# Gated mix of two linear-attention blocks: the key and value projections in five column runs instead of eight

## The chip, the cores and the metric

The kernel runs on one core of one Trainium2 chip. The metric is the device time of one execution in microseconds, as the median of several runs; lower is better.

## The reference

The input x has 2048 rows and 576 columns. Two linear-attention blocks, A and B, of 32 heads of 18 columns each read it, and a sigmoid gate mixes their outputs.

```python
def _A_ref(x, wqkv, wo):
    q, k, v = ...                      # x @ wqkv, split into 32 heads of 18
    phi = lambda t: jnp.where(t > 0, t + 1, jnp.exp(t)) + 1e-6
    pq, pk = phi(q), phi(k)
    kv = jnp.einsum("bhsd,bhse->bhde", pk, v)
    z = jnp.einsum("bhsd->bhd", pk)
    num = jnp.einsum("bhqd,bhde->bhqe", pq, kv)
    den = jnp.einsum("bhqd,bhd->bhq", pq, z)[..., None] + 1e-6
    return (num / den) ... @ wo

def _B_ref(x, wqkv, w_phi, wo):
    q, k, v = ...
    pq = jnp.einsum("bhsd,hdf->bhsf", q, w_phi)
    pk = jnp.einsum("bhsd,hdf->bhsf", k, w_phi)
    phi_q = jnp.concatenate([_softmax(pq), _softmax(-pq)], axis=-1)
    phi_k = jnp.concatenate([_softmax(pk), _softmax(-pk)], axis=-1)
    ...                                # kv, z, num, den as in A, with phi_q and phi_k

g = _sigmoid((x * gate_w).sum(-1, keepdims=True))
return g * a + (1 - g) * b
```

## The kernel before

**Tiles.** x is cut into 16 tiles of 128 rows. The host hands over x transposed, the inner dimension of 576 as five blocks of 128 (`KT`; the fifth block holds the last 64 rows twice). Every operand of a projection is split into a high part in f32r and the rest, also in f32r. `load_x` loads a tile, copies it to `xh` on ScalarE (L104) and takes the difference `xl` on GpSimd (L105). `split` does the same for a weight block: copy on ScalarE (L115), difference on VectorE or GpSimd (L117), the raw block in one of three buffers `wraw` (at the start also in halves of the three `uw` buffers).

**A projection.** `proj` (L149 to L157) adds 14 matmuls into one PSUM region: for each of the first four blocks high x times high weight, high times low, low times high, and for the fifth block, whose doubled rows hold both weight parts, two. Each has 128 rows of x as stationary operand, loaded anew, and 288 columns of a weight as moving operand. A run of columns is thus 14 matmuls.

**The key/value part.** For each tile come four projections of 576 columns, each in two runs of 288: value A, key A, key B, value B, with the weights `WAv`, `WAk`, `WBk`, `WBv` in four of five equal buffers of the pool `wp`. `WBk` is key B's weight already multiplied by `w_phi`; `fold_w` makes it on TensorE (L142) in five groups of heads, and ScalarE and VectorE write it out (L144 to L147). The values land in PSUM tiles `tr` of one bank, and ScalarE copies them into `vt` (buffer name `vo`, L233, two buffers, one a tile). The keys land in `pq`, two banks with 288 columns in each. Key A goes through `phi_elu` (ScalarE L173, VectorE L174 and L175). Key B goes through `softmax_exp`: VectorE finds maxima and minima by head and subtracts (L180, L181, L187, L188), ScalarE takes the exponential (L189), VectorE adds up by head and inverts (L191, L193); `scale_uw` then multiplies on GpSimd (L198).

**The sums.** `kv_a` and `kv_b` (L212) add the products of values and mapped keys of a tile into the two PSUM banks `bk`, which stay open over all 16 tiles. For tile t-1 they stand, in the written order, behind value A and key A of tile t. Tiles 0 and 1, and 14 and 15, have an order of their own, written out by hand.

**The query part.** It follows for the same 16 tiles, with `WBq` (folded at tile 3), `WAq`, the output weights `WoB` and `MA`, and the transposed mapped queries `uwt`, all from the same pool of five weight buffers: a later weight takes the buffer of the weight that is done. It has its own matmuls (L157 by way of `q_units`, L348, L428 to L442 transposes, L460, L490).

**What sets the order.** The kernel's text gives priorities. A scheduler places every instruction on its engine's queue by a model of the times, so the matmuls of neighbouring runs may be interleaved. Each engine then runs its queue in order and waits by semaphores. All transfers are issued on the SyncE queue (SP).

Of the kernel before, what the change touches and what calls it, by code (L numbers as in the profile page):

```python
# [11 lines left out]
ALU = mybir.AluOpType  # L12
# [11 lines left out]
VC = DH + 1  # L24
EPS = 1e-6


@with_exitstack
def tile_gated_mix(ctx, tc, xT, wAk, wAv, wBv, wAq, wkT, wqT, phi, woA, woB, out):
# [9 lines left out]
    def r(ap):  # L39
        return ap.bitcast(F32)  # L40

    def pq_tile():
        return ps.tile([P, 2, 512], F32, name="pq")

    def tr_tile():
        return ps.tile([P, 512], F32, name="tr")
# [59 lines left out]
        return xh, xl  # L106


    def w_tile():
        return wp.tile([P, 9, 578], F32R, name="W")  # L110

    def split(src, hi, lo, eng=V, raw=None):
        raw = (wraw_tile() if raw is None else raw)[:src.shape[0], :src.shape[1]]
        nc.sync.dma_start(raw, src)
        A.activation(hi, raw, AF.Copy)  # L115
        a = P - lo.shape[0] if hi.shape[0] == P else 0
        eng.tensor_tensor(lo, raw[a:], r(hi[a:]), op=ALU.subtract)  # L117

    def load_w(src, n, eng=V, raws=(None,) * KT):
        W = w_tile()  # L120
        for j in range(4):
            split(src[:, j, :], W[:, j, :n], W[:, 5 + j, :n], eng, raws[j])
        split(src[:, 4, :], W[:, 4, :n], W[64:, 4, :n], eng, raws[4])
        return W

    def fold_w(src):
        W = w_tile()
        ph = row_tile()
        nc.sync.dma_start(ph[:126, :630], phi)
        for g, nh in GROUPS:  # L130
            n = nh * DH
            c = slice(126 * g, 126 * g + n)
# [10 lines left out]
            p1v = p1[:, :504].rearrange("p (i c) -> p i c", c=126)[:, :, :n]  # L143
            A.activation(W[:, 0:4, c], p1v, AF.Copy)  # L144
            A.activation(W[:, 4, c], p2[:, :n], AF.Copy)
            V.tensor_tensor(W[:, 5:9, c], p1v, r(W[:, 0:4, c]), op=ALU.subtract)
            V.tensor_tensor(W[64:, 4, c], p2[64:, :n], r(W[64:, 4, c]), op=ALU.subtract)  # L147
        return W

    def proj(dst, x, W, c0, n):  # L150
        xh, xl = x
        steps = []
        for j in range(4):
            steps += [(xh, j, j), (xh, j, 5 + j), (xl, j, j)]
        steps += [(xh, 4, 4), (xl, 4, 4)]
        for i, (xx, j, w) in enumerate(steps):
            PE.matmul(dst, xx[:, j, :], W[:, w, c0:c0 + n], start=(i == 0), stop=(i == len(steps) - 1))  # L157

    def halves(p):
        return p[:, :, :HB]  # L160

    def heads(p):
        return p[:, :, :HB].rearrange("p a (h d) -> p a h d", d=DH)

    def bc2(t):
        return t.rearrange("p (a h) -> p a h", a=2)[:, :, :, None].to_broadcast([P, 2, 16, DH])


    def phi_elu(pq):
        f = row_tile()  # L170
        fx = f[:, :D]
        fv = fx.rearrange("p (a b) -> p a b", a=2)
        A.activation(fv, halves(pq), AF.Exp)  # L173
        V.tensor_scalar(fx, fx, 1.0, EPS, op0=ALU.min, op1=ALU.add)  # L174
        V.scalar_tensor_tensor(fv, halves(pq), 1.0 + EPS, fv, op0=ALU.add, op1=ALU.max)  # L175
        return f

    def softmax_exp(pq):
        mm = sm.tile([P, 64], F32, name="mm")
        V.tensor_reduce(mm[:, :32], heads(pq), op=ALU.max, axis=AX.X)  # L180
        V.tensor_reduce(mm[:, 32:], heads(pq), op=ALU.min, axis=AX.X)  # L181
        uw = uw_tile()

        def v4(s):
            return uw[:, s, :].rearrange("p (a h d) -> p a h d", a=2, d=DH)

        V.tensor_tensor(v4(0), heads(pq), bc2(mm[:, :32]), op=ALU.subtract)  # L187
        V.tensor_tensor(v4(1), bc2(mm[:, 32:]), heads(pq), op=ALU.subtract)  # L188
        A.activation(uw, uw, AF.Exp)  # L189
        ss = sm.tile([P, 64], F32, name="ss")  # L190
        V.tensor_reduce(ss, uw.rearrange("p s (h d) -> p (s h) d", d=DH), op=ALU.add, axis=AX.X)  # L191
        rs = sm.tile([P, 64], F32, name="rs")
        V.reciprocal(rs, ss)  # L193
        return uw, rs
# [34 lines left out]
    def do_v(t, x, W, which):  # L229
        for hf in range(2):  # L230
            pv = tr_tile()
            proj(pv[:, :HB], x, W, HB * hf, HB)
            A.activation(vt[t % 2][:, which, 16 * hf:16 * hf + 16, :DH],  # L233
                         pv[:, :HB].rearrange("p (h d) -> p h d", d=DH), AF.Copy)

    def do_pq(x, W, n=D):
        pq = pq_tile()
        proj(pq[:, 0, :HB], x, W, 0, HB)
        proj(pq[:, 1, :n - HB], x, W, HB, n - HB)
        return pq  # L240

    def do_ak(x):
        return phi_elu(do_pq(x, WAk))

    def do_bk(x, eng=G):
        uw, rs = softmax_exp(do_pq(x, WBk))
# [5 lines left out]
    WAv = load_w(wAv, D, raws=[None, None, None] + spare[:2])  # L252
    xs[1] = load_x(1)
    do_v(0, xs[0], WAv, 0)
    do_v(1, xs[1], WAv, 0)
    WAk = load_w(wAk, D, raws=spare[2:] + [None])
    f0 = do_ak(xs[0])
    f1 = do_ak(xs[1])
    kv_a(0, f0)
    WBk = fold_w(wkT)  # L260
    WBv = load_w(wBv, D)
    u0 = do_bk(xs[0])
    do_v(0, xs.pop(0), WBv, 1)
    xs[2] = load_x(2)
    kv_a(1, f1)
    u1 = do_bk(xs[1])
    kv_b(0, u0)
    do_v(1, xs.pop(1), WBv, 1)
    pend = (None, u1)
    for t in range(2, NT - 2):  # L270
        x = xs.pop(t)
        do_v(t, x, WAv, 0)
        fa = do_ak(x)
        xs[t + 1] = load_x(t + 1)
        if pend[0] is not None:
            kv_a(t - 1, pend[0])
        kv_b(t - 1, pend[1])
        uw = do_bk(x)
        do_v(t, x, WBv, 1)
        pend = (fa, uw)  # L280
        if t == 3:
            WBq = fold_w(wqT)
# [5 lines left out]
    do_v(t0, x0, WAv, 0)  # L288
    f0 = do_ak(x0)
    kv_a(t0 - 1, pend[0])  # L290
    kv_b(t0 - 1, pend[1])
    do_v(t1, x1, WAv, 0)
    f1 = do_ak(x1)
    kv_a(t0, f0)
    u0 = do_bk(x0)
    do_v(t0, x0, WBv, 1)
    kv_a(t1, f1)
    WAq = load_w(wAq, 578, G)
    u1 = do_bk(x1, V)
    do_v(t1, x1, WBv, 1)  # L300
    kv_b(t0, u0)

    def widths(p):
# [14 lines left out]

    WoB = w_tile()
# [8 lines left out]
    MA = w_tile()  # L330

    def ma_units():
        wos = []
# [25 lines left out]


    def maps_a(pa):
        f = phi_elu(pa)
# [35 lines left out]
    def q_units(t, x=None):  # L398
        x = x or load_x(t)
        pb = pq_tile()  # L400
        proj(pb[:, 0, :HB], x, WBq, 0, HB)
        yield
        proj(pb[:, 1, :HB], x, WBq, HB, HB)
        sb = softmax_exp(pb)
# [137 lines left out]
        return [wk.tile([P, KT, 256], F32R, name=n) for n in ("ath", "atl")]  # L542

    def uwt_tiles():
        u = wp.tile([126, 2, 10, 256], F32R, name="W")
        return u[:, 0], u[:, 1]

    order = [t0, t1] + list(range(NT - 2))
# [82 lines left out]
```

## Time and profile before

| | us |
|---|---|
| median of 3 runs | 625.52 (624.28 to 626.02) |
| the profiled execution | 623.18 |
| its span, first to last instruction | 621.5 |
| TensorE matmul busy, weight loads busy | 604.0, 591.5 |
| VectorE, ScalarE, GpSimd busy | 391.5, 204.7, 174.4 |

PE is TensorE's matmuls and PEld its weight loads, which overlap them; DVE is VectorE, ACT ScalarE, POOL GpSimd, SP SyncE. Matmuls are pipelined: one may start while the one before it still runs, so the time from start to start is what a matmul costs, and the duration of one in the trace holds its latency too. L157 is line 157 of the kernel before. The granted clock of TensorE is 1.000 throughout.

### The profile page before, as it was taken

Reading aid. Unit: us, or ns where it says so; the run is one execution under the profiler, and the core shown is the slowest. Engines: PE = TensorE matmul, PEld = TensorE weight load, DVE = VectorE, ACT = ScalarE, POOL = GpSimd, SP = SyncE. Lnnn points to the kernel's source line nnn. Section 1 sums busy time; section 2 is a strip of 40 time slices with the busy share of each in tenths; the row PEclk is TensorE's granted clock in tenths of the full one; section 3 lists DMA queues with packets and bytes.
Section 4 is the critical chain, followed back from the end, with each engine's and each line's share of the span. In section 5 each row is a group of like instructions: output and inputs, shape, how many; then the busy total and the mean of one; then the engine's idle time right before and its main releaser. Section 6 shows DMA issues by size and latency. Waiting matters only on the chain.

```text
span 621.5 us, 11676 instructions
## 1 busy us (share of the span) xinstructions
PE 604.0 (97%) x5000; PEld 591.5 (95%) x5000; DVE 391.5 (63%) x644; ACT 204.7 (33%) x420; POOL 174.4 (28%) x126
## 2 busy tenths in 40 slices
PE   6999999999999999999998799999999999999997
PEld 6999999999999999999997599999999999999997
DVE  6373353323323332326999998989889988889920
ACT  6342232221222222235333344243332334332331
POOL 6013221112222222245245212434133443312300
PEclk9999999999999999999999999999999999999999
DMA  8441130000000000024011101011010110000001
GB/s 285 124 142 41 44 112 3 21 22 22 22 22 24 22 22 24 22 64 122 22 38 50 35 22 40 22 42 41 20 41 22 41 42 20 20 20 20 16 24 39
DMA packets 12660, 27.94 MB, mean 45 GB/s; under 512 B 1388, under 2 KB 1388, under 8 KB 12608
## 3 DMA queue, kind: packets, MB, share of 16 engines
q1 hardware_dynamic: 12608, 27.19, 14.1%
q8 instruction: 39, 0.64, 0.4%
q14 instruction: 13, 0.11, 0.1%
HBM read 22.47 MB, written 4.72 MB: 44 GB/s over the span
## 4 chain that ended last, share of the span: by engine, by line
PE 82%; DVE 13%; ACT 2%; DMA 2%; issue 1%; SPq 0%; ACTq 0%
PE pq L157 32%; PE tr L157 19%; PE bk L490 16%; PE bk L212 5%; PE tr L460 4%; PE tr L435 2%; DVE row L384 1%; DVE dd L385 1%; DMA wraw<-wBv 1%; DVE uw L198 1%; PE tr L428 1%; DVE W L424 1%; PE pq L142 1%; DVE gg L366 1%; DVE row L175 1%; DVE den L373 1%
## 5 line engine op out<-in xcount | busy, mean ns | idle before, releaser
L157 PE MATMUL pq<-W,xh 128*128 128x288 f32 (+1 forms) x1152 | 254.3, 300 | 0.2 <-DVE den L390 0.2
L157 PEld LDWEIGHTS pq<-W,xh 128*128 128x128 f32 x1152 | 190.9, 189 | 3.1 <-PE tr L348 0.6
L157 PE MATMUL pq<-W,xl 128*128 128x288 f32 (+1 forms) x640 | 187.1, 298 | 0.0
L157 PE MATMUL tr<-W,xh 128*128 128x288 f32 x576 | 124.4, 301 | 5.8 <-ACT W L115 5.3
L105 POOL TENSOR_TENSOR xl<-xraw,xh 128x640 fp32r<-128x640 f32 x29 | 45.4, 1566 | 301.2 <-ACT xh L104 300.6
L157 PEld LDWEIGHTS pq<-W,xl 128*128 128x128 f32 x640 | 120.8, 189 | 0.2
L157 PEld LDWEIGHTS tr<-W,xh 128*128 128x128 f32 x576 | 96.7, 193 | 6.6 <-ACT W L115 5.3
L157 PE MATMUL tr<-W,xl 128*128 128x288 f32 x320 | 93.9, 299 | 0.0
L174 DVE TENSOR_SCALAR row<-row 128x576 f32<-128x576 f32 x32 | 24.4, 762 | 101.2 <-ACT row L173 101.2
L233 ACT ACTIVATE vo<-tr 128x288 f32<-128x288 f32 x64 | 25.9, 407 | 150.2 <-PE tr L157 150.2
L490 PE MATMUL bk<-W,ath 128*128 128x288 f32 x288 | 63.5, 301 | 1.1 <-ACT ath L423 0.7
L191 DVE TENSOR_REDUCE ss<-uw 128x64 f32<-128x1152 f32 x32 | 43.2, 1351 | 31.0 <-ACT uw L189 30.9
L157 PEld LDWEIGHTS tr<-W,xl 128*128 128x128 f32 x320 | 61.8, 193 | 0.0
L490 PE MATMUL bk<-W,vo 126*128 126x288 f32 x384 | 61.3, 299 | 0.0
L490 PEld LDWEIGHTS bk<-W,vo 126*128 126x128 f32 x384 | 54.0, 189 | 0.0
L180 DVE TENSOR_REDUCE mm<-pq 128x32 f32<-128x576 f32 x32 | 23.9, 748 | 47.0 <-PE pq L157 47.0
L189 ACT ACTIVATE uw<-uw 128x1152 f32<-128x1152 f32 x32 | 37.3, 1167 | 41.7 <-DVE uw L188 41.0
L490 PEld LDWEIGHTS bk<-W,ath 128*128 128x128 f32 x288 | 47.2, 189 | 1.5 <-ACT ath L423 0.9
L490 PE MATMUL bk<-W,atl 128*128 128x288 f32 x160 | 47.4, 297 | 0.0
L371 POOL TENSOR_TENSOR row<-row,z_a 128x576 f32<-128x576 f32 x16 | 30.1, 1882 | 52.5 <-DVE row L175 52.5
L460 PE MATMUL tr<-W,kb_h 126*126 126x256 f32 (+1 forms) x160 | 32.4, 283 | 1.0 <-DVE vo L465 0.8
L198 POOL TENSOR_TENSOR uw<-uw,rs 128x1152 f32<-128x1152 f32 x15 | 32.3, 2155 | 0.7 <-DVE rs L193 0.7
(138 smaller groups left out, 875.7 us busy)
## 6 DMA issues: line engine op xcount, KB each, us to landing
xraw<-xT SPq DMA_DIRECT2D x30, 320.0 KB, 3.1
out<-row SPq DMA_DIRECT2D x16, 288.0 KB, 2.1
wraw<-woA SPq DMA_DIRECT2D x6, 288.0 KB, 2.9
wraw<-wAq SPq DMA_DIRECT2D x5, 289.0 KB
wraw<-wBv SPq DMA_DIRECT2D x5, 288.0 KB, 4.2
wraw<-wkT SPq DMA_DIRECT2D x4, 315.0 KB
wraw<-wqT SPq DMA_DIRECT2D x4, 315.0 KB
uw<-wAk SPq DMA_DIRECT2D x4, 288.0 KB
```

The source lines that it names most:

```text
L105: eng.tensor_tensor(xl, raw, r(xh), op=ALU.subtract)
L157: PE.matmul(dst, xx[:, j, :], W[:, w, c0:c0 + n], start=(i == 0), stop=(i == len(steps) - 1))
L174: V.tensor_scalar(fx, fx, 1.0, EPS, op0=ALU.min, op1=ALU.add)
L180: V.tensor_reduce(mm[:, :32], heads(pq), op=ALU.max, axis=AX.X)
L189: A.activation(uw, uw, AF.Exp)
L191: V.tensor_reduce(ss, uw.rearrange("p s (h d) -> p (s h) d", d=DH), op=ALU.add, axis=AX.X)
L198: eng.tensor_tensor(u3, u3, rs[:, :, None].to_broadcast([P, 64, DH]), op=ALU.mult)
L212: PE.matmul(dst, vt[t % 2][:, which, 3 * gr:3 * gr + nh, :].rearrange("p h d -> p (h d)"), rhs, start=(t == 0 and first), stop=(t == NT - ...
L233: A.activation(vt[t % 2][:, which, 16 * hf:16 * hf + 16, :DH], pv[:, :HB].rearrange("p (h d) -> p h d", d=DH), AF.Copy)
L371: G.tensor_tensor(zw, f[:, :D], z_a, op=ALU.mult)
L460: PE.matmul(dst, kk[:n, i, :w], uu[:n, i, :256], start=(m == 0), stop=(m == 5))
L490: PE.matmul(po[:, :HB], l, w, start=(i == 0), stop=(i == len(steps) - 1))
```

## The change

The weights of the four projections of a tile, 4 x 576 = 2304 columns, are laid side by side in the order key A, value A, key B, value B, and cut into five runs of 504, 504, 504, 504 and 288 columns, which `proj` takes one at a time. A `pq` tile is used as one row of 1024 columns: run 0 fills columns 8 to 512 and run 1 columns 512 to 1016, so that key A lies in 8 to 584 and value A in 584 to 1016; runs 2 and 3 do the same, with value A's last 144 columns ahead of key B and value B's first 288 behind it; run 4, the rest of value B, goes to a `tr` tile. The maps read the 576 key columns as one stretch.

The five weight buffers become one tile `W` of 26010 columns. The runs lie first in it, then `WBq`; `WAq`, `WoB`, `MA` and `uwt` later lie over the runs. The loads write a weight in pieces, one for each run that it touches. In the steady tiles the written order becomes runs 0 and 1, the sums of the tile before, runs 2, 3 and 4. At the start key A is loaded first and run 0 of both tiles goes ahead; `kv_a` of tiles 14 and 15 stands between runs 2 and 3 of those tiles. The core of the diff:

```diff
+RUNS = [504, 504, 504, 504, 288]
+
+AK = [(0, 0, 0, 504), (1, 0, 504, 72)]
+AV = [(1, 72, 0, 432), (2, 0, 432, 144)]
+BK = [(2, 144, 0, 360), (3, 0, 360, 216)]
+BV = [(3, 216, 0, 288), (4, 0, 288, 288)]
...
-    wp = ctx.enter_context(tc.tile_pool(name="wp", bufs=5))
+    wp = ctx.enter_context(tc.tile_pool(name="wp", bufs=1))
...
+    W = wp.tile([P, 26010], F32R, name="W")
+    runs = [w_view(9 * sum(RUNS[:k]), n) for k, n in enumerate(RUNS)]
+    WBq = w_view(9 * sum(RUNS), D)
+    WAq = w_view(0, 578)
+    WoB = w_view(5202, D)
+    MA = w_view(10386, D)
+    UT = 15570
...
+    def load_runs(src, parts, raws):
+        got = []
+        for j in range(KT):
+            raw = wraw_tile() if raws[j] is None else raws[j]
+            nc.sync.dma_start(raw[:, :D], src[:, j, :])
+            got.append(raw)
+        for k, c, o, n in parts:
+            for j, raw in enumerate(got):
+                hi = runs[k][:, j, c:c + n]
+                A.activation(hi, raw[:, o:o + n], AF.Copy)
+                a, lo = (0, runs[k][:, 5 + j, c:c + n]) if j < 4 else (64, hi[64:])
+                V.tensor_tensor(lo, raw[a:, o:o + n], r(hi[a:]), op=ALU.subtract)
...
+    def run(x, k, dst):
+        proj(dst, x, runs[k], 0, RUNS[k])
...
+    def a_runs(t, x, pq=None):
+        if pq is None:
+            pq = flat(pq_tile())
+            run(x, 0, pq[:, 8:512])
+        run(x, 1, pq[:, 512:1016])
+        keep_v(t, 0, 0, pq[:, 584:1016])
+        return phi_elu(pq[:, 8:584])
...
+    def b_runs(t, x, eng=G, between=None):
+        pq = flat(pq_tile())
+        run(x, 2, pq[:, 8:512])
+        keep_v(t, 0, 24, pq[:, 8:152])
+        if between:
+            between()
+        run(x, 3, pq[:, 512:1016])
+        keep_v(t, 1, 0, pq[:, 728:1016])
+        uw, rs = softmax_exp(pq[:, 152:728])
+        pv = tr_tile()
+        run(x, 4, pv[:, :HB])
+        keep_v(t, 1, 16, pv[:, :HB])
         scale_uw(uw, rs, eng)
         return uw
...
     for t in range(2, NT - 2):
         x = xs.pop(t)
-        do_v(t, x, WAv, 0)
-        fa = do_ak(x)
+        fa = a_runs(t, x)
         xs[t + 1] = load_x(t + 1)
         if pend[0] is not None:
             kv_a(t - 1, pend[0])
         kv_b(t - 1, pend[1])
-        uw = do_bk(x)
-        do_v(t, x, WBv, 1)
-        pend = (fa, uw)
+        pend = (fa, b_runs(t, x))
...
-    f0 = do_ak(x0)
+    f0 = a_runs(t0, x0)
     kv_a(t0 - 1, pend[0])
     kv_b(t0 - 1, pend[1])
...
+    f1 = a_runs(t1, x1)
+    u0 = b_runs(t0, x0, between=lambda: kv_a(t0, f0))
+    load_w(WAq, wAq, 578, G)
+    u1 = b_runs(t1, x1, V, between=lambda: kv_a(t1, f1))
     kv_b(t0, u0)
```

More of the change, by code (lines that the diff above doesn't have):

```diff
@@ L106, in load_x, with w_view @@
         return xh, xl
-    def w_tile():
-        return wp.tile([P, 9, 578], F32R, name="W")
+    W = wp.tile([P, 26010], F32R, name="W")
+    def w_view(at, n, a=9):
+        return W[:, at:at + a * n].rearrange("p (a c) -> p a c", a=a)
+    runs = [w_view(9 * sum(RUNS[:k]), n) for k, n in enumerate(RUNS)]
[4 more added lines that the diff above has]
+    UT = 15570
     def split(src, hi, lo, eng=V, raw=None):
@@ L117, in split, with load_w, fold_w @@
         eng.tensor_tensor(lo, raw[a:], r(hi[a:]), op=ALU.subtract)
[L119 to L127 removed]
+    def load_runs(src, parts, raws):
[10 more added lines that the diff above has]
+                V.tensor_tensor(lo, raw[a:, o:o + n], r(hi[a:]), op=ALU.subtract)
+    def load_w(W, src, n, eng=V):
+        for j in range(4):
+            split(src[:, j, :], W[:, j, :n], W[:, 5 + j, :n], eng)
+        split(src[:, 4, :], W[:, 4, :n], W[64:, 4, :n], eng)
+    def fold_w(src, parts):
         ph = row_tile()
@@ L142, in fold_w @@
                 PE.matmul(dst, raw[:n, P * i:P * i + P], ph[:n, 126 * g:126 * g + n], start=True, stop=True)
[L143 to L148, printed above, removed]
+            p1v = p1[:, :504].rearrange("p (i c) -> p i c", c=126)
+            for w, c0, o, m in parts:
+                lo, hi = max(126 * g, o), min(126 * g + n, o + m)
+                if lo >= hi:
+                    continue
+                c, q = slice(c0 + lo - o, c0 + hi - o), slice(lo - 126 * g, hi - 126 * g)
+                A.activation(w[:, 0:4, c], p1v[:, :, q], AF.Copy)
+                A.activation(w[:, 4, c], p2[:, q], AF.Copy)
+                V.tensor_tensor(w[:, 5:9, c], p1v[:, :, q], r(w[:, 0:4, c]), op=ALU.subtract)
+                V.tensor_tensor(w[64:, 4, c], p2[64:, q], r(w[64:, 4, c]), op=ALU.subtract)
     def proj(dst, x, W, c0, n):
@@ L227, in kv_b, with flat, keep_v @@
                      uw[:, :, 54 * gr:54 * gr + DH * nh], p == 1)
[L229 to L246, printed above, removed]
+    def flat(p):
+        return p.rearrange("p a c -> p (a c)")
+    def run(x, k, dst):
+        proj(dst, x, runs[k], 0, RUNS[k])
+    def keep_v(t, which, h0, src):
+        n = src.shape[1] // DH
+        A.activation(vt[t % 2][:, which, h0:h0 + n, :DH], src.rearrange("p (h d) -> p h d", d=DH), AF.Copy)
+    def a_runs(t, x, pq=None):
[17 more added lines that the diff above has]
+        keep_v(t, 1, 16, pv[:, :HB])
         scale_uw(uw, rs, eng)
@@ L251, in tile_gated_mix @@
     spare = [u[:, i] for u in (uw_tile(), uw_tile(), uw_tile()) for i in range(2)]
-    WAv = load_w(wAv, D, raws=[None, None, None] + spare[:2])
+    load_runs(wAk, AK, [None, None, None] + spare[:2])
     xs[1] = load_x(1)
[L254 to L258, printed above, removed]
-    kv_a(0, f0)
[L260 to L264, printed above, removed]
+    first = []
+    for t in range(2):
+        pq = flat(pq_tile())
+        run(xs[t], 0, pq[:, 8:512])
+        first.append(pq)
+    load_runs(wAv, AV, spare[2:] + [None])
+    f0, f1 = [a_runs(t, xs[t], first[t]) for t in range(2)]
+    fold_w(wkT, [(runs[k], c, o, n) for k, c, o, n in BK])
+    load_runs(wBv, BV, [None] * KT)
+    u0 = b_runs(0, xs.pop(0))
+    xs[2] = load_x(2)
+    kv_a(0, f0)
+    u1 = b_runs(1, xs.pop(1))
     kv_a(1, f1)
-    u1 = do_bk(xs[1])
     kv_b(0, u0)
-    do_v(1, xs.pop(1), WBv, 1)
     pend = (None, u1)
@@ L544, in uwt_tiles @@
     def uwt_tiles():
-        u = wp.tile([126, 2, 10, 256], F32R, name="W")
+        u = W[:126, UT:UT + 5120].rearrange("p (a g n) -> p a g n", a=2, g=10)
         return u[:, 0], u[:, 1]
```

49 lines of the change are left out of this document (20 added, 29 removed).

## The prediction

> **What bounds the kernel now.** I read the page first: TensorE is busy nearly everywhere and owns the chain that ended last.
>
> ```profile
> span 621.5 us, 11676 instructions
> PE 604.0 (97%) x5000; PEld 591.5 (95%) x5000; DVE 391.5 (63%) x644; ACT 204.7 (33%) x420; POOL 174.4 (28%) x126
> PE 82%; DVE 13%; ACT 2%; DMA 2%; issue 1%; SPq 0%; ACTq 0%
> ```
>
> Then the stages. The columns of the next fence are busy time of TensorE, its weight loads, VectorE, ScalarE and GpSimd in three windows: the start (tiles 0 and 1), the steady tiles 2 to 13, and the last two key/value tiles.
>
> ```profile
> 0.00:51.53 51.53, 45.53 (x366) 44.24 (x366) 29.78 (x44) 24.42 (x43) 16.54 (x29) 1.00 0.56 172
> 51.53:266.60 215.07, 215.07 (x1978) 211.16 (x1976) 75.71 (x108) 52.49 (x96) 45.38 (x25) 1.00 0.10 29
> 266.60:300.01 33.41, 33.41 (x309) 32.47 (x307) 17.41 (x32) 13.60 (x23) 15.40 (x11) 1.00 0.31 87
> ```
>
> In the steady tiles TensorE has no idle time at all, the clock is fully granted and the other engines are a third busy or less. So the change is worth there what it takes from or adds to TensorE, and a new wait counts in full. One steady tile, by line (first the projections, L157, then the key-value sums, L212):
>
> ```profile
> 181.97:198.89 16.92, 15.19 (x112) 14.96 (x112) 1.00 0.07 21
> 181.97:198.89 16.92, 1.86 (x46) 1.70 (x44) 1.00 0.07 21
> ```
>
> A tile is 16.92 us: 112 projection matmuls of 288 columns (8 runs of 14) and 1.9 us of sums. The whole gain must come from the first row.
>
> **What a matmul costs by its width.** Matmuls overlap in the trace, so durations mislead; the distance between starts is the price. Timeline rows of TensorE, with start, time, and count:
>
> ```profile
> 429.94 0.29 PE L460 MATMUL tr<-W,kb_h 126*126 126x256 f32 x1
> ...
> 431.24 0.28 PE L460 MATMUL tr<-W,kb_h 126*126 126x256 f32 x1
> 431.36 0.30 PE L490 MATMUL bk<-W,ath 128*128 128x288 f32 x1
> ...
> 440.62 1.77 PE L490 MATMUL bk<-W,vo 126*128 126x288 f32 x12
> 442.22 0.30 PE L490 MATMUL bk<-W,atl 128*128 128x288 f32 x1
> ...
> 320.98 1.13 PE L348 MATMUL tr<-wraw,ath 128*128 128x288 f32 x4
> ...
> 361.94 0.60 PE L435 MATMUL tr<-ident,uw 128*126 128x128 f32 x4
> ...
> 42.28 0.30 PE L157 MATMUL pq<-W,xl 128*128 128x288 f32 x1
> 43.09 0.40 PE L157 MATMUL tr<-W,xh 128*128 128x288 f32 x1 [0.52 <-ACT vo L233]
> ```
>
> - Width 256 in f32r: twelve matmuls from 429.94 to 431.36, 1.42/12 = 118.3 ns each.
> - Width 288 in f32r: twelve from 440.62 to 442.22, 1.60/12 = 133.3 ns. The steady tile agrees: (16.92 - 1.9)/112 = 134.
> - Plain f32 (L348, 288 columns, median duration 406 ns in the row below): (1.13 - 0.406)/3 = 241 ns; L435 with 128 columns: (0.60 - 0.272)/3 = 109 ns. A line through these two has 0.825 ns a column and 3.7 ns that do not depend on the width.
> - The matmul at 42.28 has no successor, and so no weight load beside it, until 43.09, and lasts 0.30 like those that have one. Weight loads cost nothing here; removing them brings nothing.
>
> ```profile
> L348 PE MATMUL tr<-wraw,ath x28: 403/406/510, 321.0 to 346.6; 128*128 128x288 f32 x28
> L435 PE MATMUL tr<-ident,uw x120: 270/272/328, 356.6 to 598.2; 128*126 128x128 f32 x120
> L460 PE MATMUL tr<-W,kb_h x160: 274/280/386, 362.5 to 606.1; 126*126 126x256 f32 x128, 72*80 72x256 f32 x32
> ```
>
> **The change, part by part.**
>
> *Projections.* Per tile 8 x 14 matmuls of 288 columns become 4 x 14 of 504 and 14 of 288. The columns stay 2304, so only the width-independent part c of a matmul is saved: 3 per step, 14 steps, 16 tiles, 672 matmuls in all. No row has 504 columns, so c is bounded. From the f32r pair: 133.3 - 118.3 = 15.0 ns for 32 columns is 0.469 a column, which leaves c = -1.7 ns; taken at its word, 504 columns cost 234.6 and a step 4 x 234.6 + 133.3 = 1071.7 against 8 x 133.3 = 1066.4, a loss of 5.3 ns x 224 steps = 1.2 us. At the other end, if f32r streamed at half of f32's 241 ns and all the rest were fixed, c = 133.3 - 120.6 = 12.7 ns and the gain is 672 x 12.7 = 8.5 us. Against that end: 256 columns would then cost 133.3 - 32 x 0.419 = 119.9, and the row says 118.3. The f32 rows give c = 3.7 ns, 2.5 us. I take the middle between none and 3.7, 1.9 ns, since the f32r pair is nearest in kind and says none: a 504-column matmul costs 1.9 + 131.4 x 504/288 = 231.9 ns, a step 1060.9, and the gain is 672 x 1.9 = 1.3 us.
>
> A rule to weigh against this. The Trainium skill, page "TensorE: Matmul & The Clock Gate", section "Back-to-back issue gap", gives a warm gap of N/2.4 + 2.5 ns; by it the saving would be 672 x 2.5 = 1.7 us, but it makes 288 columns cost 122.5, where the row has 133.3, so the f32r stream is slower than this rule says and the small fixed part is what trace and rule share.
>
> *Evacuation.* ScalarE still copies values four times a tile (432, 144, 288 and 288 columns instead of four of 288), and the key maps read the same 576 columns, now in one piece across two banks. ScalarE is busy 52.49 of 215.07 us; cost nothing on the path.
>
> *The order of the tile.* Before, key-B is followed by 28 matmuls of value-B, 28 of value-A and 28 of key-A before the sums of its softmax. Now only run 4 and the next tile's runs 0 and 1 stand between. The chain that they cover:
>
> ```profile
> 202.94 0.76 DVE L180 TENSOR_REDUCE mm<-pq 128x32 f32<-128x576 f32 x1 [3.73 <-PE pq L157]
> 205.77 1.17 ACT L189 ACTIVATE uw<-uw 128x1152 f32<-128x1152 f32 x1 [0.51 <-DVE uw L188]
> 206.97 1.35 DVE L191 TENSOR_REDUCE ss<-uw 128x64 f32<-128x1152 f32 x1 [1.29 <-ACT uw L189]
> 208.36 0.55 DVE L193 RECIPROCAL rs<-ss 128x64 f32<-128x64 f32 x1
> 207.65 1.56 POOL L105 TENSOR_TENSOR xl<-xraw,xh 128x640 fp32r<-128x640 f32 x1 [13.25 <-ACT xh L104]
> 209.16 2.15 POOL L198 TENSOR_TENSOR uw<-uw,rs 128x1152 f32<-128x1152 f32 x1
> 214.02 0.76 PE L212 MATMUL bk<-row,vo 128*57 128x54 f32 x21
> 214.65 1.24 PE L212 MATMUL bk<-uw,vo 128*57 128x108 f32 x21
> ```
>
> From the last key-B matmul (202.94) the scaled weights are ready at 209.16 + 2.15 = 211.31, 8.4 us later; TensorE reads them at 214.6, 11.7 us later: 84 x 0.133 = 11.2 and half a microsecond of kv_a. Slack 3.3 us. After the change the cover is 14 x 0.133 + 28 x 0.232 + 0.5 = 8.9 us, slack 0.5. I cost it at nothing, but the cover is nearly gone. What frees the next x tile now is the end of run 4, 1.9 us after run 3, so GpSimd's xl of 1.56 us should run well before its scale.
>
> *The start.* Weights come as the same number of DMAs and bytes on SP's queue, key-A first instead of value-A. For value-B all five raw tiles are asked for together with three buffers, so the last two transfers wait for the pieces of the first. ScalarE and VectorE get more and smaller pieces: 15 more each for the loads, and one group of the fold split in two.
>
> ```profile
> L115 ACT ACTIVATE W<-wraw x9: 684/686/687, 4.6 to 37.5; 128x576 fp32r<-128x576 f32 x9
> L117 DVE TENSOR_TENSOR W<-wraw,W x9: 755/759/761, 5.3 to 39.3; 128x576 fp32r<-128x576 f32 x7, 64x576 fp32r<-64x576 f32 x2
> L144 ACT ACTIVATE W<-pq x3: 397/592/593, 25.8 to 31.6; 128x504 fp32r<-128x504 f32 x2, 128x288 fp32r<-128x288 f32 x1
> PE tr L157 <- ACT W L115: 5.3, 1, 5.3
> PE tr L157 <- ACT vo L233: 0.5, 1, 0.5
> ```
>
> On ScalarE 288 columns take 0.397 and 504 take 0.592, so 0.0009 a column and 0.14 fixed: 15 pieces add 2.1 us on ScalarE and about as much on VectorE, which are busy 24.4 and 29.8 of the first 51.5 us. TensorE first waits 5.3 us for the first weights, unchanged, and then 0.5. Its own work up to tile 2 has the same columns. Before, the last value-B piece is written at 39.3 + 0.8 = 40.1 us (the L117 row), and TensorE's only later wait is the 0.5 us. After, it would come about 1 us later for the extra pieces, unless the fold, which now waits for 288 fewer columns of A-work, starts earlier; TensorE has run 2 of the second tile (14 x 0.232 = 3.2 us) to do meanwhile. I cost it at 0, with 2 us to either side.
>
> *The end of the key/value part.* One weight tile of 26010 columns replaces five buffers, and the later weights overlay the runs: WAq starts only when run 1 of the last tile is done (2.8 us later than value-A was: 28 x 0.232 against 28 x 0.133), and the last rows of WoB when run 2 is. GpSimd does both, and then the scale:
>
> ```profile
> 285.43 1.21 POOL L117 TENSOR_TENSOR W<-wraw,W 126x576 fp32r<-126x576 f32 x1 [0.50 <-ACT W L115]
> 286.60 2.15 POOL L198 TENSOR_TENSOR uw<-uw,rs 128x1152 f32<-128x1152 f32 x1
> 291.01 1.26 PE L212 MATMUL bk<-uw,vo 128*57 128x108 f32 x22
> ```
>
> The scale ends at 288.75 and is read at 291.01, a slack of 2.3 us that a delay of 2.8 would just pass, by 0.5 us. WAq itself is read only by the query part, after 291 us, and WoB later still. The last softmax also moves 1.9 us nearer the end. Cost: 0, with up to 2 us above.
>
> **Sum.** 1.3 us less and the rest at nothing. The profiled execution took 623.18 us (span 621.5 and 1.7 around it), which gives 621.9; it was faster than the median of the runs, 625.52, so there the forecast is 624.2.
>
> **The rivals.**
>
> 1. A fixed part larger than I took, up to 12.7 ns: 8.5 us, 617.0 us. For it: the widths 256 and 288 lie close and in different stages, and 1.6 ns between 118.3 and 119.9 is all that decides. Against: the sign of that difference. The same Trainium skill section also has sustained figures of 81 ns at width 128 and 131 at 512; by them the change would save 40 us or so, and the row of 288 columns at 133.3 contradicts them.
>
> 2. The sums wait for the softmax weights in every steady tile, which ends on the slow side. The place is kv_b behind GpSimd's scale; it decides once the chain is over 0.5 us longer. If xl goes in front of the scale at the wrong moment it adds up to 1.56, so about 1 us of stall a tile; over 13 tiles 13 us, 637 us; at a fifth of that, 627. Against it: xl's early release.
>
> 3. The start or the hand-over to the query part loses 2 to 3 us, with the stream gaining 1.3: 626 to 627.
>
> **How the numbers follow.** This measurement can tell about 0.3% (1.9 us) from no change. My forecast, streaming in proportion with c from -1.7 to 3.7, has 0.53: 622 to 627 of its own, of which 0.14 faster, 0.31 within, 0.08 slower. Rival 1 has 0.27, all faster. Rival 2 has 0.13, slower. Rival 3 has 0.07, of which 0.05 slower. Faster 0.41, same 0.33, slower 0.26. The range goes from the end of rival 1, 616.5, to 628.5, which leaves out the bulk of rival 2.
>
> **What would show it.** Right: starts of 504-column matmuls 230 to 234 ns apart and a steady tile of 16.8 to 16.9 us with no TensorE wait. Starts 223 apart and a tile near 16.35 show rival 1. An idle time of TensorE ended by GpSimd's L198 copy line in each tile shows rival 2. Idle before 51 us or between 270 and 345 us shows rival 3. The forecast is wrong if the width-independent part is large, or if the order that came out places the sums ahead of their weights.

## The result and the profile after

The changed kernel takes 641.57 us (median of 4 runs, 640.4 to 643.61) against 625.77 us for the kernel before beside it (624.28 to 626.11): a ratio of 1.0261, with a 95% interval of 1.023 to 1.0292. That is 15.8 us slower, outside the range of the forecast. The profiled execution took 640.4 us. In the changed kernel the projections' matmul is L186, the sums' L247, the value copies L272, the softmax's first step L215 and its scale L233 (before: L157, L212, L233, L180, L198).

From its page, the span, the busy times and the shares of the chain that ended last:

```profile
span 638.7 us, 10405 instructions
PE 609.8 (95%) x4328; PEld 552.6 (87%) x4328; DVE 395.8 (62%) x661; ACT 204.4 (32%) x437; POOL 173.7 (27%) x126
PE 80%; DVE 12%; DMA 3%; ACT 2%; POOL 1%; issue 1%; SPq 0%; DVEq 0%; POOLq 0%; ACTq 0%
```

672 matmuls are gone, and TensorE is busy 5.8 us longer. Four windows of TensorE show where; the columns are width, busy time, instructions, granted clock, DMA share and GB/s. First the kernel before, then the changed one:

```profile
12.00:100.00 88.00, 87.33 (x775) 1.00 0.32 92
100.00:265.00 165.00, 165.00 (x1505) 1.00 0.07 21
265.00:400.00 135.00, 128.51 (x1043) 1.00 0.16 48
400.00:621.50 221.50, 216.51 (x1662) 1.00 0.08 29
```

```profile
12.00:100.00 88.00, 82.39 (x547) 1.00 0.31 90
100.00:265.00 165.00, 165.00 (x1100) 1.00 0.06 19
265.00:400.00 135.00, 121.98 (x879) 0.96 0.16 45
400.00:638.70 238.70, 233.79 (x1796) 1.00 0.09 29
```

Width less busy time is idle time. It grows between 12 and 100 us from 0.67 to 5.61 us, and between 265 and 400 us (the last two tiles and the first query tiles) from 6.49 to 13.02. In that third window the granted clock falls to 0.96, and this too is a loss: three stretches of 3.41 us ran at half clock, and each lost half of that, 5.1 us together. The sum, 4.9 + 6.5 + 5.1 = 16.5, is nearly the whole difference of the spans, 17.2. The steady tiles have no idle time, as before.

**The width itself.** Timeline rows of TensorE in the changed kernel: 28 matmuls of 504 columns lie between the first and the last of these rows.

```profile
272.79 0.62 PE L186 MATMUL pq<-W,xh 128*128 128x504 f32 x2
...
279.20 0.61 PE L186 MATMUL pq<-W,xh 128*128 128x504 f32 x2
```

6.41/28 = 229 ns each; the forecast said 231.9. With 133 at 288 columns a step costs 4 x 229 + 133 = 1049 ns against 1066, so the stream gains 17 ns x 224 = 3.9 us, not 1.3. And yet the steady tile got no shorter. The rows are: one tile's projections, then its sums.

```profile
202.29:219.27 16.98, 15.20 (x71) 12.23 (x70) 1.00 0.06 16
202.29:219.27 16.98, 2.06 (x45) 1.78 (x45) 1.00 0.06 16
```

**Where the order changed.** In a steady tile of the changed kernel the sums stand in two places, and run 3 and the scale of the weights come late. Rows of one tile; of the projections only the last two matmuls of run 3 are shown (214.37 and 214.59: a run goes two high and one low four times and ends with one high and one low):

```profile
206.52 0.29 ACT L272 ACTIVATE vo<-pq 128x144 f32<-128x144 f32 x1 [2.88 <-PE pq L186]
211.94 1.26 PE L247 MATMUL bk<-uw,vo 128*57 128x108 f32 x22
213.29 0.41 ACT L272 ACTIVATE vo<-tr 128x288 f32<-128x288 f32 x1 [6.47 <-PE bk L247]
214.37 0.39 PE L186 MATMUL pq<-W,xh 128*128 128x504 f32 x1
214.59 0.39 PE L186 MATMUL pq<-W,xl 128*128 128x504 f32 x1
214.84 0.74 ACT L111 ACTIVATE xh<-xraw 128x640 fp32r<-128x640 f32 x1 [1.14 <-PE pq L186]
215.49 0.40 ACT L272 ACTIVATE vo<-pq 128x288 f32<-128x288 f32 x1
215.92 0.76 DVE L215 TENSOR_REDUCE mm<-pq 128x32 f32<-128x576 f32 x1 [10.41 <-ACT vo L272]
219.27 0.80 PE L247 MATMUL bk<-row,vo 128*57 128x54 f32 x22
222.22 2.15 POOL L233 TENSOR_TENSOR uw<-uw,rs 128x1152 f32<-128x1152 f32 x1 [4.99 <-DVE rs L228]
```

Value columns and key-B columns now share the two-bank PSUM tile `pq`. In the program, the softmax's first reading on VectorE waits for the last value copy out of that tile on ScalarE, and run 3 waits for the copy of 144 columns out of its first bank. ScalarE took its copies in this order: the one at 213.29 had stood 6.47 us behind the sums (it needs the value buffer that they free), then came the x copy, which waits until run 3 is done with the x tile, then the copy that VectorE wanted. The list of waits has this as VectorE's largest in the changed kernel (total, times, longest); in the kernel before, the softmax's first step had only the wait for the projection (second fence):

```profile
DVE mm L215 <- ACT vo L272: 136.3, 15, 11.1
```

```profile
DVE mm L180 <- PE pq L157: 47.0, 17, 3.7
```

A wait in this list is put down to whatever ended it. Run 3 itself ends only at 214.59 + 0.39 = 214.98 us, so of the 10.41 us before the softmax only the last 0.9 belong to ScalarE's copies; it is 0.93 in each steady tile, against 0.04 between the last key-B matmul and the softmax in the kernel before. The rest is the late place of run 3. The scheduler put run 4 and nine matmuls of run 0, both of the next tile, between run 2 and run 3, and the key-B sums into run 3. TensorE has no idle time from this in the steady tiles. Nor are the split sums of this order the copies' doing: in copies_last2 below the copies come last, and the tile is still 16.97 us long with the sums in two places.

At the end of the key/value part there is no next tile, and the runs 4 are used up (the last one starts at 270.84). The rows there:

```profile
292.69 0.41 ACT L272 ACTIVATE vo<-pq 128x288 f32<-128x288 f32 x1
293.14 0.76 DVE L215 TENSOR_REDUCE mm<-pq 128x32 f32<-128x576 f32 x1 [11.14 <-ACT vo L272]
300.46 2.14 POOL L233 TENSOR_TENSOR uw<-uw,rs 128x1152 f32<-128x1152 f32 x1 [6.28 <-DVE rs L228]
302.66 1.66 PE L247 MATMUL bk<-uw,vo 128*57 128x108 f32 x22 [2.68 <-POOL uw L233]
```

Tile 14's softmax starts at 293.14, in the kernel before at 279.02; 5.3 us of these 14 were brought along from earlier (the key-A sums of tile 13 begin at 270.11, before at 264.80). Of the other 8.8 us, 7.3 are the later place of run 3, which ends at 291.62, and 1.5 are ScalarE's queue, where copies of the output weights stand ahead of the value copy. TensorE waits 2.68 us for it, and VectorE has both softmaxes and the first query tile's at once, so the query part's waits grow as well.

### The profile page after: what moved, and what is told of

Its sections match the earlier page's. It is cut to its first block, busy times and chain, and to the rows that moved or that the text cites. A ratio compares the mean times of both kernels' runs of the same rounds, so it can differ in the third digit from the quotient of the medians.

```text
span 638.7 us, 10405 instructions
## 1 busy us (share of the span) xinstructions
PE 609.8 (95%) x4328; PEld 552.6 (87%) x4328; DVE 395.8 (62%) x661; ACT 204.4 (32%) x437; POOL 173.7 (27%) x126
## 4 chain that ended last, share of the span: by engine, by line
PE 80%; DVE 12%; DMA 3%; ACT 2%; POOL 1%; issue 1%; SPq 0%; DVEq 0%; POOLq 0%; ACTq 0%
PE pq L186 45%; PE bk L528 16%; PE tr L186 5%; PE bk L247 4%; PE tr L498 4%; PE tr L473 2%; DVE dd L423 1%; PE tr L466 1%; DMA wraw<-woB 1%; DVE row L422 1%; DVE ss L226 1%; DVE uw L233 1%; DVE row L210 1%; DMA uw<-wAk 1%; DVE mm L215 1%
## 5 line engine op out<-in xcount | busy, mean ns | idle before, releaser
L186 PE MATMUL pq<-W,xh 128*128 128x504 f32 (+2 forms) x1152 | 318.1, 352 | 11.1 <-ACT W L144 5.1
L186 PEld LDWEIGHTS pq<-W,xh 128*128 128x128 f32 x1152 | 205.0, 192 | 36.8 <-ACT W L144 5.4
L186 PE MATMUL pq<-W,xl 128*128 128x504 f32 (+2 forms) x640 | 221.7, 350 | 0.0
L186 PEld LDWEIGHTS pq<-W,xl 128*128 128x128 f32 x640 | 122.7, 192 | 13.3
L215 DVE TENSOR_REDUCE mm<-pq 128x32 f32<-128x576 f32 x32 | 23.9, 748 | 137.2 <-ACT vo L272 136.3
L233 POOL TENSOR_TENSOR uw<-uw,rs 128x1152 f32<-128x1152 f32 x15 | 32.3, 2154 | 79.0 <-DVE rs L228 70.2
L209 DVE TENSOR_SCALAR row<-row 128x576 f32<-128x576 f32 x32 | 26.4, 825 | 28.9 <-ACT row L208 28.9
L272 ACT ACTIVATE vo<-pq 128x432 f32<-128x432 f32 (+2 forms) x48 | 19.4, 404 | 66.5 <-PE pq L186 66.4
L111 ACT ACTIVATE xh<-xraw 128x640 fp32r<-128x640 f32 x30 | 22.1, 738 | 56.1 <-PE pq L186 54.3
L415 POOL TENSOR_TENSOR row<-row,den 128x576 f32<-128x576 f32 x16 | 20.0, 1249 | 47.7 <-DVE den L413 21.4
L186 PE MATMUL tr<-W,xh 128*128 128x288 f32 x144 | 32.5, 301 | 0.4 <-DVE W L177 0.4
L461 ACT ACTIVATE W<-tr 126x512 fp32r<-126x512 f32 (+1 forms) x44 | 23.2, 528 | 24.0 <-DVE atl L482 15.8
```

Source lines behind the costliest of these rows:

```text
L215: V.tensor_reduce(mm[:, :32], as_heads(src), op=ALU.max, axis=AX.X)
L233: eng.tensor_tensor(u3, u3, rs[:, :, None].to_broadcast([P, 64, DH]), op=ALU.mult)
L461: A.activation(h, src, AF.Copy)
```

## The experiments

Theory W: the value copies, which now stand ahead of the softmax in the same tile and in ScalarE's queue, delay run 3 and the softmax; the forced order splits the sums and starves TensorE at the hand-over. Rivals: the width itself; the text order of the last two tiles (sums between runs, the query weights loaded between them); the start and the query fold. The kernel before beside these runs took 626.0 to 626.7 us. Gains are given as differences of the medians; taken through the ratios they differ by up to 1.5 us.

**width_undone.** The changed kernel with narrower matmuls:

```
 def run(x, k, dst):
-    proj(dst, x, runs[k], 0, RUNS[k])
+    proj(dst[:, :HB], x, runs[k], 0, HB)
+    if RUNS[k] > HB:
+        proj(dst[:, HB:], x, runs[k], HB, RUNS[k] - HB)
```

> The changed kernel in everything but the width: each run of 504 columns is issued as 288 and 216 columns, so 896 more matmuls. If the loss comes from the new arrangement (tiles, copies, order) and not from the width, the time stays above the changed kernel's 641.6 us: a pair costs 133 ns plus an estimated 102 ns (133 less 72 columns at the 0.44 ns per column between 288 and 504) against 229, so 896 x 6 ns = 5 us more, 647 us (643 to 649). If wide matmuls are what costs, it falls back to the kernel before, 624 to 628.

Measured 645.75 us (1.0307, 1.029 to 1.0324): the width is not the loss. This is not yet its price, since other widths gave another order; joined_width_undone has that.

**copies_last.** Run 3 directly behind run 2, then the softmax, then both copies:

```
-        keep_v(t, 0, 24, pq[:, 8:152])
         if between:
             between()
         run(x, 3, pq[:, 512:1016])
-        keep_v(t, 1, 0, pq[:, 728:1016])
         uw, rs = softmax_exp(pq[:, 152:728])
+        keep_v(t, 0, 24, pq[:, 8:152])
+        keep_v(t, 1, 0, pq[:, 728:1016])
```

> The changed kernel with one thing moved: in b_runs both value copies out of the two-bank tile are issued after the softmax, so that VectorE reads the tile as soon as run 3 has ended and run 3 does not wait for the copy of 144 columns. Theory of the waits (softmax and run 3 stand behind ScalarE's copies of the same tile): the softmax's idle time in the steady tiles (136 us in 15) goes, the weights are ready for the sums earlier, the last two tiles no longer stand late; 630 to 634 us. Rival, the text order of the last two tiles (sums between runs, query weights loaded between them) does it: 639 to 642. Rival, the start and the folds: no more than 1 us changes, 640.5 to 642.

Measured 632.62 us (1.0114, 1.0077 to 1.0151). In this kernel, and in handover_plain and copies_handover, a key-A sum of the last two tiles reads eight heads of values ahead of their copy, so their times are those of kernels with one wait less there; copies_last2 and handover_plain2 have the sums behind the copies.

**handover_plain.** Sums and query weights of the last two tiles taken out from between the runs:

```
-    u0 = b_runs(t0, x0, between=lambda: kv_a(t0, f0))
-    load_w(WAq, wAq, 578, G)
-    u1 = b_runs(t1, x1, V, between=lambda: kv_a(t1, f1))
+    u0 = b_runs(t0, x0)
+    kv_a(t0, f0)
+    kv_a(t1, f1)
+    u1 = b_runs(t1, x1, V)
+    load_w(WAq, wAq, 578, G)
```

> The changed kernel with the last two tiles written plainly: run 2 to run 4 of tile 14, both key-A sums, run 2 to run 4 of tile 15, and the query weights loaded only then. The value copies stay ahead of the softmax. Rival, the text order of the last two tiles: 9 us of the 16 are lost there, so 632 to 634. Theory of the waits: the copies still hold the softmax, so no more than 3 us comes back, 638 to 642; loading the query weights later may cost some of it.

Measured 638.19 us (1.0183, 1.015 to 1.0216).

**copies_handover.** Both edits.

> The two edits together: value copies after the softmax, and the last two tiles written plainly. Theory of the waits: about what the copies alone give, 629 to 634. If copies and order each carry a part, lower than either alone by about the sum of the two gains, and no lower than 627, since the start's 5 us are left in.

Measured 634.2 us (1.0149, 1.0105 to 1.0194): no lower than copies_last, against the sum of the parts.

**copies_last2.** As copies_last, but the sums of the last two tiles come behind the copy that they need:

```
-        if between:
-            between()
         run(x, 3, pq[:, 512:1016])
         uw, rs = softmax_exp(pq[:, 152:728])
         keep_v(t, 0, 24, pq[:, 8:152])
+        if between:
+            between()
         keep_v(t, 1, 0, pq[:, 728:1016])
```

> As copies_last, but with the key-A sums of the last two tiles put behind the copy of the eight heads that they read (copies_last let them read the buffer before it). Theory of the waits: the same 631 to 634 us, since the gain is the softmax's earlier start. Rival, copies_last gained because its last sums were let off a wait: 637 to 641.

Measured 634.2 us (1.0128, 1.01 to 1.0156): 7.4 us back. Besides the copies, this edit puts the key-A sums of tiles 14 and 15 behind run 3; joined_copies_first, below, is free of that. VectorE waits for the projection again, and tile 14's softmax, whose run 3 now follows its run 2 at once, is on time:

```profile
DVE mm L215 <- PE pq L186: 83.1, 18, 7.0
287.08 0.76 DVE L215 TENSOR_REDUCE mm<-pq 128x32 f32<-128x576 f32 x1 [2.56 <-PE pq L186]
```

From the key-A sums of tile 13 (271.91) that is 15.2 us; it was 14.2 before and 23.0 in the changed kernel. The idle time from 265 to 400 us is 6.66 us (135.00 less 128.34), that of the kernel before. In the steady tiles nothing is gained: a tile takes 16.97 us, and between 100 and 265 us TensorE changes 38 times between projections and sums (37 in the changed kernel). What is left is the start (6.50 us idle up to 100 us) and three half-clock stretches, two at the query fold and one in the first query tiles.

**handover_plain2.** As handover_plain, with tile 15's sums behind its own runs:

```
     u0 = b_runs(t0, x0)
     kv_a(t0, f0)
-    kv_a(t1, f1)
     u1 = b_runs(t1, x1, V)
+    kv_a(t1, f1)
     load_w(WAq, wAq, 578, G)
```

> As handover_plain, but each key-A sum of the last two tiles comes behind its own tile's runs, so that it reads what it should; copies still ahead of the softmax. Rival, the text order of the last two tiles carries the loss: 632 to 634. Theory of the waits: 637 to 641, since the softmaxes still stand behind the copies.

Measured 633.86 us (1.0117, 1.0097 to 1.0138): the rival's number, 7.7 us back, and theory W's expectation missed. But not by the rival's way: VectorE's wait that ends with the copies is still 136.3 us, and tile 14's softmax is still 23.3 us behind the sums of tile 13 (2.3 of them behind its own run 3). Four runs of the query projections (two in the changed kernel) now stand ahead of tile 14's key-B sums; idle time from 265 to 400 us fell to 8.31 us, and no half-clock stretch lies there. So the written order of the last two tiles carries part of the loss too.

**start_folds.** Tile 1's x loaded behind both weights; the query fold one group a tile:

```
-    xs[1] = load_x(1)
-    first = []
-    for t in range(2):
-        pq = flat(pq_tile())
-        run(xs[t], 0, pq[:, 8:512])
-        first.append(pq)
     load_runs(wAv, AV, spare[2:] + [None])
-    f0, f1 = [a_runs(t, xs[t], first[t]) for t in range(2)]
+    xs[1] = load_x(1)
+    f0 = a_runs(0, xs[0])
+    f1 = a_runs(1, xs[1])
...
-        if t == 3:
-            fold_w(wqT, [(WBq, 0, 0, D)])
+        if 3 <= t < 8:
+            fold_w(wqT, [(WBq, 0, 0, D)], GROUPS[t - 3:t - 2])
```

> The changed kernel with two other edits, both outside the steady tiles and the hand-over: tile 1's x is loaded after both key-A and value weights, so that tile 0's two runs come wholly before tile 1's and its ELU lies beside them; and the query fold is done one group per tile in tiles 3 to 7 in place of five groups in tile 3. If the start and that fold are where 5 us went (1.70, 1.10, 0.66, 0.41, 1.42 and 0.57 us of waits), 636 to 638.5. If the waits only move on, 640 to 642.

Measured 631.97 us (1.0092, 1.0056 to 1.0128): 9.6 us back, far more than the 3 to 5 expected. Idle time up to 100 us fell from 5.61 to 2.70 us, as meant. The rest came 200 us later, where nothing was edited: from 265 to 400 us the idle time fell from 13.02 to 8.09, and the three half-clock stretches are gone. The spread fold seems to have moved the phase of the scheduler's pattern (start_only, below, has the rest of this edit and not this effect; the fold by itself was not run in the changed kernel), and run 3 of tile 14 now came ahead of run 2 of tile 15.

**copies_handover_start.** copies_last2, handover_plain2 and start_folds together.

> The three edits together (copies_last2, handover_plain2, start_folds). If the parts add up and the width's gain of 3.9 us is real, 624 to 628: the loss of 16 us is undone, less what the split sums of each tile cost (0.3 us a tile). If something else of the arrangement costs, 629 or more.

Measured 627.74 us (1.0035, 1.0018 to 1.0052): 13.8 of the 15.8 us are back. The single gains, 7.4 + 7.7 + 9.6, add to 24.7, because each of the three also removed much of the same idle time (13.02 us from 265 to 400 us fell to 6.66, 8.31 and 8.09) and of the same half-clock stretches there (three became one, none and none).

**sums_joined.** In addition, both sums of the tile before behind run 3:

```
+        def sums(t=t, pend=pend):
+            if pend[0] is not None:
+                kv_a(t - 1, pend[0])
+            kv_b(t - 1, pend[1])
-        pend = (fa, b_runs(t, x))
+        pend = (fa, b_runs(t, x, between=sums))
```

> copies_handover_start (627.7 us) with the sums of the tile before put behind run 3 of each steady tile, key-A sums and key-B sums in one place. If TensorE pays for each change between projections and sums, as the period of 16.97 us against 16.68 (16.92 less the width's 0.24) says, ten to twelve tiles give 0.3 us each back: 623.5 to 626, under the kernel before (626.3). If the split costs nothing and the period comes from something else, 627 to 629.

Measured 626.14 us against 626.73 (0.9994, 0.9978 to 1.0009), the same as before. The steady tile at last shows the width (projections, then sums, of one tile):

```profile
202.69:219.32 16.63, 14.90 (x71) 12.30 (x70) 1.00 0.08 22
202.69:219.32 16.63, 1.87 (x44) 1.70 (x45) 1.00 0.08 22
```

16.63 us against 16.92 before. The split tile of the changed kernel took 0.35 us more, 16.98: put down to its two more changes between projections and sums, an estimate of 0.17 us each. They ate the stream's gain.

**joined_width_undone.** sums_joined with the narrower matmuls of width_undone.

> sums_joined with each run of 504 columns issued as 288 and 216 columns: 896 more matmuls. By the starts in the traces (133 ns and an estimated 102 ns against 229), 5 us more than sums_joined; if width is worth nothing once the order is right, the same time within 1 us.

Measured 640.87 us (1.0225, 1.0211 to 1.0239), 14.7 us more than sums_joined, not 5. The expectation's 102 ns for 216 columns was wrong; 14 of them run from the first to the last of these starts:

```profile
206.02 0.38 PE L186 MATMUL pq<-W,xh 128*128 128x216 f32 x2
...
207.58 0.44 PE L186 MATMUL pq<-W,xh 128*128 128x288 f32 x2
```

1.56/14 = 111 ns, so a pair is 244 against 229, and 896 x 15 ns = 13.4 us, most of the 14.7. Width_undone's 4.2 us was this price less some 10 us that its own order happened to save: its profile has 9.0 us less idle time than the changed kernel's (2.74 us up to 100 us, 6.94 from 265 to 400) and two half-clock stretches fewer.

**before_folds_spread.** A control: the kernel before with its fold spread in the same way.

```
-        if t == 3:
-            WBq = fold_w(wqT)
+        if t == 3:
+            WBq = w_tile()
+        if 3 <= t < 8:
+            fold_w(wqT, WBq, GROUPS[t - 3:t - 2])
```

> A control: the kernel before, with only the query fold done one group per tile in tiles 3 to 7. Its trace shows no wait at that fold. If start_folds gained by taking away waits that the change had brought, nothing is gained here: within 1 us of the kernel before. If spreading the fold is good in itself, 2 us or more faster.

Measured 625.9 us (0.9991, 0.9979 to 1.0003): nothing. The gain of start_folds belongs to the changed kernel's order.

**joined_copies_first.** sums_joined with the copies put back ahead of the softmax; in the text the softmax thereby also stands behind the sums:

```
         run(x, 2, pq[:, 8:512])
+        keep_v(t, 0, 24, pq[:, 8:152])
         run(x, 3, pq[:, 512:1016])
-        uw, rs = softmax_exp(pq[:, 152:728])
-        keep_v(t, 0, 24, pq[:, 8:152])
         if between:
             between()
         keep_v(t, 1, 0, pq[:, 728:1016])
+        uw, rs = softmax_exp(pq[:, 152:728])
```

> sums_joined (626.1 us) with the value copies of b_runs put back ahead of the softmax, nothing else. Theory of the waits: run 3 waits for the copy of 144 columns again and the softmax for that of 288; tile 14's softmax comes late and TensorE waits at the hand-over and in the first query tiles: 630 to 636. Rival, the copies' place is worth nothing in a good order, and the loss was of the text order alone: 625 to 628.

Measured 633.65 us (1.0128, 1.01 to 1.0155): 7.5 us for the place of two copies, in an order that is otherwise as fast as the kernel before (the two versions of sums_joined run beside it, below, took 626.15 and 625.89). The wait that ends with the copies is back, though the softmax starts only 0.5 to 0.9 us behind its run 3, and the steady window gets fewer matmuls done. The first two rows are this kernel's, the third is sums_joined's:

```profile
DVE mm L215 <- ACT vo L272: 91.3, 16, 8.6
100.00:265.00 165.00, 165.00 (x1104) 1.00 0.11 31
```

```profile
100.00:265.00 165.00, 165.00 (x1147) 1.00 0.11 33
```

TensorE is busy all of it in both, but changes 56 times between projections and sums in these 165 us, against 30: by the estimate above 26 x 0.17 = 4.4 us. With another half-clock stretch (1.7) and 1.3 + 1.1 us of idle time in the first and third window this makes 8.5 of the 10.4 us between the two profiled spans (633.1 and 622.7).

**joined_fold_once** is sums_joined with `if t == 3:` and the whole fold back, **start_only** the changed kernel with only start_folds' first edit, and **joined_elu_first** sums_joined with

```
-        keep_v(t, 0, 0, pq[:, 584:1016])
-        return phi_elu(pq[:, 8:584])
+        f = phi_elu(pq[:, 8:584])
+        keep_v(t, 0, 0, pq[:, 584:1016])
+        return f
```

> sums_joined with the query fold back in tile 3, all five groups at once. If that fold's waits (1.42 and 0.57 us in the changed kernel, 3.0 in copies_last2, with two windows of halved clock after them) are a loss of their own, 629 to 632. If only the start mattered in start_folds, 625.5 to 627.5.

> sums_joined with phi_elu issued ahead of the copy of 432 columns in a_runs as well. The Exp starts 0.5 us earlier on ScalarE and the copy 0.6 us later. The ELU is on no wait of TensorE in the steady tiles: 625.5 to 627 (nothing). If the copy has to wait for VectorE's second read of the tile, run 0 of the next tile could be held: 628 or more.

> The changed kernel with tile 1's x loaded after both weights, so that tile 0's runs come wholly ahead of tile 1's; folds, copies and hand-over as in the changed kernel. By its own wait (1.70 us for the ELU) 639.5 to 640.5. If start_folds' gain of 9.7 us came from here, 632 to 634; if nothing, 641 to 643.

Measured 626.15 us (1.0002, 0.9986 to 1.0018), 625.89 (1.0002, 0.9991 to 1.0013) and 639.18 (1.0223, 1.0187 to 1.0258), in this order. Once the copies are last, the fold's place is worth nothing; the ELU's place is worth nothing; the start by itself is some 2.4 us (its six executions go from 637.29 to 645.92), so the larger part of start_folds came with the spread fold.

## Why the prediction was wrong

- *Projections, 1.3 us.* Right in kind, undersized: 229 ns a matmul, 17 ns a step, 3.9 us. In an order without split sums a steady tile gains 0.29 us (16.92 to 16.63). Rival 1 (223 ns, a tile of 16.35) is out.
- *Weight loads cost nothing.* The row at 42.28 showed a duration, not a distance between starts. At 256, 288 and 504 columns the starts lie on one line (0.444 ns a column and 5), so the load shows in none of them. At 216 it may: 111 ns, where the line gives 101. The Trainium skill, page "TensorE: Matmul & The Clock Gate", section "LDWEIGHTS (loading the stationary operand)", gives the number of columns / 1.2 ns, an estimate of 107 ns for 128 columns. The row of 216 columns is within 4 ns of that, though no run here took the loads away.
- *Evacuation, "cost nothing on the path".* This is the step that failed. It counted the copies and ScalarE's busy time (a quarter of the steady window) and not who stands behind them: four copies, as before, but two now come out of the tile that the softmax reads and run 3 fills. Directly the softmax loses 0.93 us a steady tile by this and 1.5 in tile 14. The larger part comes by the order that the scheduler then writes, with run 3 apart from run 2. joined_copies_first prices it: 7.5 us.
- *The order of the tile, "the cover is nearly gone".* The slack of 0.5 us was worked out for the written order. The order that came out was another: no wait of TensorE in the steady tiles, but twice as many changes between projections and sums (37 in the steady window, 19 before). In this order they are there with the copies last, too (38 in copies_last2); joining the sums in the text took them down to 30. Rival 2, a stall in every tile, did not happen.
- *The start, 0 plus or minus 2.* 4.9 us more idle time up to 100 us, 2.0 of it at the query fold in tile 3, which this term left out. Tile 0's and tile 1's run 1 follow the arriving weights in turns and end together, so the first key-A sums wait for the ELU (first row); the query fold waits for its own pieces (second row), and key B's fold for a transfer (third row), 1.1 us where it was 0.2 before. From the list of TensorE's waits:

```profile
PE bk L247 <- DVE row L210: 1.7, 1, 1.7
PE pq L167 <- DVE W L177: 1.4, 1, 1.4
PE tr L167 <- DMA wraw<-wkT: 1.1, 1, 1.1
```

- *The end of the key/value part, 0 with up to 2.* 6.5 us of idle time and 5.1 of half clock, in part the copies' doing. Rival 3 named both places and sized them at 2 to 3 us together.

That the copies' place costs some 7.5 us is shown in two orders, and it is made of different things in them: in the changed kernel of idle time at the hand-over (13.02 to 6.66 us), in the joined order for the larger part of more changes in the steady tiles. How the remaining 8 us share themselves among the start, the written end and the phase of the scheduler's pattern is not settled, since each edit moves the order of all that follows. No version beat the kernel before: against the width's gain stand, in the profile of sums_joined, 0.8 us more idle time up to 100 us, 30 changes against 19 in the steady window (1.9 us by the estimate) and one half-clock stretch (1.7 us). The last is no steady term: the profile of the kernel before has none, but most of its other executions show granted clocks of 0.994 to 0.997, and most of sums_joined's 0.994 to 0.999.

## What to carry to other kernels

When two results are packed into one PSUM tile, ask which reader the next engine waits for, and issue the urgent reader first; two copies of 0.3 and 0.4 us, on an engine that is busy a third of the time, cost 7.5 us by their place. Read a list of waits with care: it named the copies for 136 us, of which they held up the reader for about 1 us a tile, while the rest was the matmuls' own place. Judge a merged layout by the order that comes out of it (how often the matmul stream changes, what waits on the tile), not by the busy times. And where a scheduler writes the order, test an edit inside a good arrangement: in the broken one, three different edits each seemed to be half the cure.

## What the runs showed of the hardware

**The clock looks at fixed windows.** Two windows of 3.41 us each in the changed kernel, a waiting one and the one behind it, twice; then three in a row of the kernel before:

```profile
299.96:303.37 3.41, 0.73 (x17) 1.00 0.00 0
303.37:306.78 3.41, 3.41 (x22) 0.50 0.00 0
330.67:334.08 3.41, 1.39 (x5) 1.00 0.00 0
334.08:337.49 3.41, 3.41 (x15) 0.50 0.00 0
```

```profile
339.46:342.87 3.41, 1.45 (x8) 1.00 0.32 87
342.87:346.28 3.41, 1.54 (x9) 1.00 0.32 96
346.28:349.69 3.41, 3.34 (x21) 1.00 0.00 0
```

In each trace the half-clock stretches lie on a grid of 3.41 us. Over the 17 traces, without the first and the last 20 us of each, all 20 windows in which TensorE idled over 2.0 us were followed by one at half clock; of 12 with 1.6 to 2.0 us, 8 were; below that only windows that already ran at half clock. So waits of 1.51 and 0.75 us, with 2.02 us of them in the window from 330.67, cost another 1.7, while a wait of 3.83 us in the kernel before lay across two windows and cost nothing more. Where the windows lie against the waits differs from one execution to the next: the four of the changed kernel show granted clocks from 0.985 (643.61 us) to 0.991 (640.40 us). The Trainium skill, page "TensorE: Matmul & The Clock Gate", section "What's actually happening", gives free-running windows of 3413 ns, and the grid agrees; its advice, in the section "Why this matters for your kernels", is to avoid idle gaps over about 3 us; here the runs differ, since every such stretch of the changed kernel followed waits of under 2.7 us.
